# First layer's turns as integers and q's second order on ScalarE, block inputs in their own buffer, later first blocks and no saved credit in a fused attention and two-layer kernel

## The chip, the cores and the metric

The kernel runs on one core of a Trainium2 chip. The metric is the device time of one execution in microseconds. The core has TensorE (PE in the rows: matmuls; PEld: its weight loads), VectorE (DVE), ScalarE (ACT), GpSimd (POOL) and SyncE (SP), whose queue issues every DMA of this kernel, one after the other.

## What is computed

An attention with queries that are the means of neighbouring pairs, then two dense layers. The weights arrive in double width (64 bit), q, k and v in single, and the output is single.

```python
def reference(q, k, v, w_in1, w_out1, w_in2, w_out2):   # B, H, S, D = 4, 8, 1152, 64
    qp = q.reshape(B, H, S // 2, 2, D).mean(axis=3)
    s = qp @ k.transpose(0, 1, 3, 2) / np.sqrt(D)
    a = np.exp(s - s.max(-1, keepdims=True))
    x = (a / (a.sum(-1, keepdims=True) + 1e-9)) @ v       # to rows of 8 * 64 = 512
    h = x @ w_in1;  x = (h * np.cos(h)) @ w_out1          # 512 -> 2048 -> 512
    h = x @ w_in2;  return (h / (1 + np.exp(-h))) @ w_out2
```

## The kernel before

Every product of near single precision is made from half-precision parts: a number is split into a high part and the rest (the second order), and three products are summed. Splits are ScalarE (high part), then VectorE or POOL (the rest).

The attention runs over 4 batches of 4 pairs of heads (heads j and j + 4), and each pair has 9 tiles of 128 queries (the ninth holds 64 of either head): 144 tiles. A tile goes through TensorE (`tile_scores`), VectorE (eviction with the minimum, L568, L573), ScalarE (exponential, L576, and its high part, L582), POOL (the rest, L150, three pieces), one transpose by DMA of both parts (L589, hlT) and TensorE again (`tile_pv`, L600 and L604). The ring of `hl` has 4 buffers, scores have one PSUM buffer for each of their two halves, and the second product of a tile follows 4 tiles later (`LAG`).

The next pair is prepared meanwhile. `pair_prep` finds scales and splits q, k and v; it and the loads (`pair_loads`) are generators of which the tile loop takes a step every second call of `advance` (four calls a tile, 36 a pair). For q, `qn` holds four column sets: for e = 0 the high part beside the rest, for e = 1 the rest beside the high part (the two halves of the contraction meet k's high part and rest). All of it goes through one DMA transpose (L515), as k does (L525).

When a batch is done its 512 whole rows are two blocks of 256 tokens; its remaining 64 rows wait for a ninth block. `block_steps` scales and splits a block (`x_split`, whose `xn` is a buffer of the ring `hl`), transposes it (xT) and puts it into `blocks_q`, in batches 1 to 3 only 40 calls of `advance` (10 tiles) later.

`layer1` is a generator of units. For each chunk f of 128 of the 2048 columns there is one unit of 12 matmuls into PSUM (`g1_unit`; two chunks share a buffer, of which there are two), and 12 chunks later one for the second product (`g2_unit1`). After each second chunk ScalarE evicts two chunks as turns, h / 2 pi, into `hk` (L701). After each fourth, VectorE makes the turns' distance to the nearest whole number: add a quarter, add and subtract 1.5 * 2^23 (L713, L714, into a buffer of the tag `tt`). ScalarE takes the sine (L720), VectorE multiplies and rounds (L723, L728), POOL makes the rest (L150, gl). A block's output y32 takes a buffer of `tt`, too, and goes to DRAM (L752). `tt`, `hk`, `gh` and `gl` have two buffers each.

`share` runs units: each call adds a credit, of which at most 4 are kept, and every unit costs one. A tile makes two calls in batches 1 to 3. After the last tile the rest of the first layer runs with the preparation of the second layer's weights (`layer2_weight_steps`); then the second layer's blocks follow, by TensorE mostly.

The framework orders all instructions by a list scheduler over modelled times, with the program's order and hand-set priorities (`ahead`) as keys; each engine then runs its own list in order.

Of the kernel before, what the change touches and what calls it, by code (L numbers as in the profile page):

```python
# [20 lines left out]
EXP_MASK = 0x7F800000  # L21
MAGIC = 12582912.0
TINY = 2.0**-50
# [3 lines left out]
PSH = 15.0  # L27
NB_N, NB_SC, NB_H, NB_T, NB_S = 2, 4, 4, 4, 5
LOW_HL, LOW_G, LOW_W = 3, 2, 2
X_LAG = 40  # L30
W1_BUFS, WT_BUFS = 3, 3
# [18 lines left out]
def attention_moe_moe_kernel(ctx, tc, q, k, v, w_in1, w_out1, w_in2, w_out2, out):  # L50
# [23 lines left out]
    halfpi = const.tile([128, 1], F32, name="halfpi")  # L74
    floor3 = const.tile([128, 1], F32, name="floor3")

    def make_consts():
        nc.vector.memset(mean, 2.0**-7)
        nc.vector.memset(halfpi, math.pi / 2)
        nc.vector.memset(floor3, 2.0**-14 - 0.5)  # L80

    GW = 256
# [390 lines left out]
    def pair_prep(at, P):  # L473
# [32 lines left out]

        qn = at.src.tile([128, 2, NQ, 2, D], F16, tag="kn", name="qn", bufs=NB_N)
        for e in range(2):
            nc.scalar.activation(out=qn[:, e, :, e, :], in_=qs, func=AF.Copy, scale=s[:, 0:1])
        nc.vector.scalar_tensor_tensor(  # L510
            out=qn[:, 0, :, 1, :], in0=qs, scalar=s[:, 0:1], in1=qn[:, 0, :, 0, :], op0=ALU.mult, op1=ALU.subtract
        )
        nc.vector.tensor_copy(qn[:, 1, :, 0, :], qn[:, 0, :, 1, :])
        qT = at.p.tile([128, 2, NQ, 128], F16, tag="qT", name="qT", bufs=2)
        nc.sync.dma_start_transpose(  # L515
            out=qT.rearrange("p e n k -> p (e n) k"), in_=qn.rearrange("p e n s d -> p (e n s d)")
        )
        P.qT = [qT[:, e] for e in range(2)]
        yield
        kn = at.src.tile([128, 2, KC, 2, D], F16, tag="kn", name="kn", bufs=NB_N)  # L520
        for i in range(2):
# [8 lines left out]
        for i in range(2):  # L530
            do_v(i)
            yield

    segs = [(o, min(512, S - o)) for o in range(0, S, 512)]
# [122 lines left out]
    def x_split(at, mp, x32, i, blk, w):  # L657

        m = small.tile([128, 1], F32, name="xm", tag="xm")
        absmax(m, x32, AX.XY)  # L660
        yield
        s = small.tile([128, 1], F32, name="xs", tag="xs")
        u = small.tile([128, 1], F32, name="xu", tag="xu")
        yield from early(scale_steps(m, ps_h, (s, u), 14), P_CH)
        blk.c = x_scale_consts(w, s, u, True)
        xn = at.p.tile([128, 2, 2, DM], F16, tag="hl", name="xn", bufs=NB_H)
        nc.scalar.activation(out=xn[:, 0], in_=x32, func=AF.Copy, scale=s)
        nc.vector.scalar_tensor_tensor(out=xn[:, 1], in0=x32, scalar=s, in1=xn[:, 0], op0=ALU.mult, op1=ALU.subtract)
        yield
        blk.T = mp.p.tile([128, 2, 2, NC, 128], F16, tag="x%d" % i, name="xT", bufs=1)  # L670
        nc.sync.dma_start_transpose(
            out=blk.T.rearrange("p e t c k -> p (e t c) k"), in_=xn.rearrange("p e t d -> p (e t d)")
        )
        blk.xh = lambda c: blk.T[:, 0, :, c, :]
        blk.xl = lambda c: blk.T[:, 1, :, c, :]
# [15 lines left out]
    def g1_evac(mp, w, blk, f, first):  # L691
# [3 lines left out]
        if first:  # L695
            if f % 4 == 1:
                blk.hk = mp.p.tile([128, 4, GW], F32, tag="hk", name="hk", bufs=NB_HK)
            o = blk.hk[:, (f % 4) - 1:(f % 4) + 1, :]
        else:
            o = blk.view(f - 1, 2)  # L700
        nc.scalar.activation(  # L701
            out=o, in_=blk.hp, func=AF.Copy if first else AF.Silu, scale=blk.c.a[:, g:g + 1]
        )

    def g_cos_begin(mp, blk):
# [5 lines left out]
        blk.g.append((G.gh, G.gl))  # L711
        G.t = t = mp.p.tile([128, 4, GW], F32, tag="tt", name="tt", bufs=NB_TT)
        nc.vector.tensor_scalar(out=t, in0=G.hk, scalar1=0.25, scalar2=MAGIC, op0=ALU.add, op1=ALU.add)  # L713
        nc.vector.scalar_tensor_tensor(out=t, in0=t, scalar=MAGIC, in1=G.hk, op0=ALU.subtract, op1=ALU.subtract)  # L714
        return G
# [165 lines left out]
    if True:  # L881
# [12 lines left out]
        state = Weights()  # L894
        state.mp = None
        state.ng, state.tail = 0, False
# [51 lines left out]
        def share(x):  # L948
            if state.mp is None:
                return  # L950
            state.credit = min(state.credit + x, 4.0)
            while state.credit >= 1 and next(units, False):
                state.credit -= 1
# [31 lines left out]
        def block_steps(b, i):  # L985
# [3 lines left out]
            yield from early(x_split(at, state.mp, x32.pop((b, i)), i, blk, W1), P_X)  # L989
            if b:  # L990
                for _ in range(X_LAG):
                    yield
            blocks_q.append(blk)
# [8 lines left out]
        def block_done(b, i):  # L1002
            if state.mp is None:
                finish(wg)
                wst_stack.close()
                state.mp = moe_pools(moe_stack)
            xgens[b, i] = block_steps(b, i)
            bg.append(xgens[b, i])
# [41 lines left out]
        for n, (b, j) in enumerate(pairs):  # L1050
# [13 lines left out]
            else:  # L1064
                at.src_stack.close()
                w2st_stack = ExitStack()
                w2st = w2st_stack.enter_context(tc.tile_pool(name="w2st", bufs=1, reuse_waits="tile"))
# [203 lines left out]
```

## Time and profile before

| | us |
|---|---|
| median of 3 runs | 1358.67 (1353.96 to 1359.51) |
| the profiled execution, own time | 1361.32 |
| its span, first to last instruction | 1359.5 |
| mean granted clock of TensorE | 0.916 |
| end of the attention in it | about 829 |
| TensorE without a gap from | about 1059 |

The profile gives the busy time of each engine, the windows its distribution over time, and the groups what each line costs and what ended the idle time before it. A wait is named by engine and line, with the releaser behind an arrow. DMA share is the mean busy share of the 16 DMA engines.

### The profile page before, as it was taken

The page shows a single profiled execution, that of the slowest core. Times are in us where ns is not written, and L with a number is a line of the kernel's source. Part 1 is how long each engine was busy: PE and PEld are TensorE (multiplying, and loading weights), DVE is VectorE, ACT ScalarE, POOL GpSimd, SP SyncE. Part 2 cuts the span into 40 slices and gives each one's busy share as a digit, 9 for nine tenths or more (in the row PEclk, how much of TensorE's full clock was granted, in tenths as well). Part 3 has the DMA queues.
Part 4 walks back from the last instruction along what each step waited for, and adds up shares of the span by engine and source line. Part 5 has one row for each costly group of instructions (what it writes and reads, how often), then busy time and mean ns, then how long its engine had stood idle before and what let it go on. Part 6 is the DMA issues. An engine that isn't in the chain of part 4 may idle for free. (4 is left out here: it accounts for less than half of the span.)

```text
span 1359.5 us, 26737 instructions
## 1 busy us (share of the span) xinstructions
PE 1146.0 (84%) x10668; PEld 914.5 (67%) x10668; DVE 981.6 (72%) x1927; ACT 870.0 (64%) x1061; POOL 705.1 (52%) x624
## 2 busy tenths in 40 slices
PE   1564565888988679998898999899999999999998
PEld 0333343666766456675676677788788888888887
DVE  6896978877877777795787795986757755444483
ACT  3896888778777777885788774634546633333352
POOL 1688686688668576875768673533667400000000
PEclk9677676989999888998999999999899999999999
DMA  9999999889799999998999975413344000000001
GB/s 270 210 229 219 224 242 208 152 159 175 139 191 186 195 201 202 191 162 161 164 181 190 197 174 100 128 60 75 82 97 106 32 30 27 9 16 17 17 32 32
DMA packets 509597, 186.29 MB, mean 137 GB/s; under 512 B 465952, under 2 KB 484384, under 8 KB 509472
## 3 DMA queue, kind: packets, MB, share of 16 engines
q1 hardware_dynamic: 509472, 184.59, 65.7%
q8 instruction: 83, 1.36, 0.4%
q14 instruction: 42, 0.34, 0.1%
HBM read 66.58 MB, written 9.44 MB: 56 GB/s over the span
## 5 line engine op out<-in xcount | busy, mean ns | idle before, releaser
L150 POOL TENSOR_TENSOR hl<-sc,hl 128x384 f16<-128x384 f32 x432 | 453.8, 1081 | 145.3 <-ACT hl L582 110.1
L568 DVE TENSOR_SCALAR_CACHE_REDUCE sc<-sp,psu 128x512 f32<-128x512 f32 (+1 forms) x288 | 229.7, 808 | 78.1 <-PE sp L549 66.9
L549 PE MATMUL sp<-kT,qT 128*128 128x512 f16 (+1 forms) x768 | 195.3, 373 | 83.5 <-DVE sc L568 58.7
L685 PEld LDWEIGHTS <-ih 128*128 128x128 f16 x2304 | 226.3, 100 | 45.7 <-issue 13.8
L600 PE MATMUL pv<-vt,hlT 128*128 128x130 f16 (+1 forms) x1440 | 194.6, 236 | 73.8 <-DMA hlT<-hl 68.2
L576 ACT ACTIVATE sc<-sc,nb 128x1152 f32<-128x1152 f32 x144 | 179.4, 1249 | 76.8 <-DVE nb L573 69.7
L600 PEld LDWEIGHTS <-hlT 128*128 128x128 f16 (+1 forms) x1440 | 144.6, 109 | 106.3 <-DMA hlT<-hl 80.9
L685 PE MATMUL h<-ys,ih 128*128 128x256 f16 x1152 | 195.6, 274 | 4.1 <-ACT gs L701 4.1
L685 PE MATMUL h<-xT,ih 128*128 128x256 f16 x1024 | 186.3, 277 | 5.1 <-ACT hk L701 2.1
L604 PE MATMUL pv<-vt,hlT 128*128 128x65 f16 (+1 forms) x1440 | 184.7, 206 | 0.0
L582 ACT ACTIVATE hl<-sc 128x1152 f16<-128x1152 f32 x144 | 165.2, 1154 | 26.2 <-DMA hlT<-hl 20.0
L549 PEld LDWEIGHTS <-qT 128*128 128x128 f16 x768 | 77.1, 109 | 150.9 <-issue 102.5
L740 PE MATMUL y<-gh,oh 128*128 128x256 f16 x576 | 162.8, 283 | 6.8 <-ACT y L749 6.8
L740 PE MATMUL y<-gl,oh 128*128 128x256 f16 x576 | 163.1, 283 | 1.9 <-POOL gl L150 1.9
L740 PE MATMUL y<-gh,ol 128*128 128x256 f16 x576 | 162.6, 282 | 0.0
L854 PEld LDWEIGHTS <-op 128*128 128x128 f16 x1512 | 147.9, 98 | 18.0 <-issue 0.6
L685 PE MATMUL h<-ys,il 128*128 128x256 f16 x576 | 157.7, 274 | 0.0
L604 PEld LDWEIGHTS <-hlT 128*128 128x128 f16 (+1 forms) x1440 | 141.2, 107 | 14.6 <-issue 7.1
L685 PE MATMUL h<-xT,il 128*128 128x256 f16 x512 | 141.8, 277 | 0.0
L150 POOL TENSOR_TENSOR gl<-tt,gh 128x512 f16<-128x512 f32 (+1 forms) x60 | 97.3, 1637 | 79.7 <-DVE gh L728 61.0
L740 PEld LDWEIGHTS <-oh 128*128 128x128 f16 x1152 | 115.4, 102 | 30.8 <-issue 10.3
L685 PEld LDWEIGHTS <-il 128*128 128x128 f16 x1152 | 114.2, 99 | 16.9 <-issue 0.4
(310 smaller groups left out, 1967.6 us busy)
## 6 DMA issues: line engine op xcount, KB each, us to landing
wst<-in_moe_w_in_dram SPq DMA_DIRECT2D x16, 1024.0 KB, 6.1
stk<-in_k_dram SPq DMA_DIRECT2D x32, 288.0 KB, 4.2
stv<-in_v_dram SPq DMA_DIRECT2D x32, 288.0 KB, 4.4
stq<-in_q_dram SPq DMA_DIRECT2D x32, 256.0 KB, 3.1
wst<-in_moe_w_out_dram SPq DMA_DIRECT2D x8, 1024.0 KB, 6.4
wst<-in_moe_w_out_dram SPq DMA_DIRECT2D x16, 512.0 KB, 6.0
ydr<-y SPq DMA_DIRECT2D x9, 512.0 KB, 3.3
y32b<-ydr SPq DMA_DIRECT2D x9, 512.0 KB, 3.3
```

The source lines that it names most:

```text
L150: last = nc.gpsimd.tensor_tensor(out=lo[:, o:o + w], in0=x[:, o:o + w], in1=hi[:, o:o + w], op=ALU.subtract)
L549: nc.tensor.matmul(sp[:, o - a:o - a + n], P.qT[e][:, t, :], kT[:, o:o + n], start=(e == 0), stop=(e == 1))
L568: nc.vector.tensor_scalar(out=T.sc[:, a:z], in0=sp, scalar1=T.P.su, scalar2=None, op0=ALU.mult, op1=ALU.min, accum_out=mx[:, x:x + 1],)
L576: nc.scalar.activation(out=T.sc, in_=T.sc, func=AF.Exp, scale=-1.0, bias=nb)
L582: nc.scalar.activation(out=hi, in_=T.sc, func=AF.Copy)
L600: nc.tensor.matmul(G.pv[r, T.gi], T.hlT[:, 0, c, r], P.vt[i][:, c], start=(c == 0), stop=(c == KC - 1), skip_group_check=True,)
L604: nc.tensor.matmul(G.pv[r, T.gi, 0], T.hlT[:, 1, c, r], P.vt[i][:, c, 0], start=False, stop=(c == KC - 1), skip_group_check=True,)
L685: nc.tensor.matmul(hp, wt[:, c, f * 128:(f + 1) * 128], xt(c), start=(i == 0), stop=(i == 3 * NC - 1), skip_group_check=True,)
L740: nc.tensor.matmul(blk.y[:, oc, :], wt[:, f, oc * 128:(oc + 1) * 128], gt[:, f % 4, :], start=(f == 0 and e == 0 and oc % 2 == 0), stop=(f ...
L854: nc.tensor.matmul(bank, t[:, e, c, :], wt[:, c, :], start=start, stop=True, skip_group_check=True)
```

## The change

- `g1_evac` reads each PSUM buffer of the first layer twice: as before into `hk`, and with a quarter added, converted to 32-bit integers, into a buffer of `tt` that is now claimed at the second chunk of four. VectorE's two instructions become one, integer minus turns.
- `qn` holds q's high part and rest once, in a buffer of its own, and the transpose takes 9 blocks, not 18. The e = 1 half of `qT` is made from the e = 0 half by two ScalarE copies that swap the upper and lower 64 partitions, as a last step of `pair_prep`. `kn` has one buffer.
- `xn` has a buffer in a pool of its own, as long as that pool is open (until the last pair of batch 3 begins; there the steps of batch 2's blocks are finished first). After that it uses `hl` as before.
- `X_LAG` is 20 calls for batch 0 (before: none) and 40 for the others.
- When `share` finds no unit to run, the credit is set to 0.

```diff
-        qn = at.src.tile([128, 2, NQ, 2, D], F16, tag="kn", name="qn", bufs=NB_N)
-        for e in range(2):
-            nc.scalar.activation(out=qn[:, e, :, e, :], in_=qs, func=AF.Copy, scale=s[:, 0:1])
-        nc.vector.scalar_tensor_tensor(
-            out=qn[:, 0, :, 1, :], in0=qs, scalar=s[:, 0:1], in1=qn[:, 0, :, 0, :], op0=ALU.mult, op1=ALU.subtract
-        )
-        nc.vector.tensor_copy(qn[:, 1, :, 0, :], qn[:, 0, :, 1, :])
+        qn = at.src.tile([128, NQ, 2, D], F16, tag="qn", name="qn", bufs=1)
+        split(qn[:, :, 0, :], qn[:, :, 1, :], qs, s[:, 0:1], False)
         qT = at.p.tile([128, 2, NQ, 128], F16, tag="qT", name="qT", bufs=2)
-        nc.sync.dma_start_transpose(
-            out=qT.rearrange("p e n k -> p (e n) k"), in_=qn.rearrange("p e n s d -> p (e n s d)")
-        )
+        nc.sync.dma_start_transpose(out=qT[:, 0], in_=qn.rearrange("p n s d -> p (n s d)"))
...
-        kn = at.src.tile([128, 2, KC, 2, D], F16, tag="kn", name="kn", bufs=NB_N)
+        kn = at.src.tile([128, 2, KC, 2, D], F16, tag="kn", name="kn", bufs=1)
...
+        for x, y in ((slice(0, 64), slice(64, 128)), (slice(64, 128), slice(0, 64))):
+            nc.scalar.activation(out=qT[x, 1], in_=qT[y, 0], func=AF.Copy)
+        yield
...
-        xn = at.p.tile([128, 2, 2, DM], F16, tag="hl", name="xn", bufs=NB_H)
+        if state.xp is None:
+            xn = at.p.tile([128, 2, 2, DM], F16, tag="hl", name="xn", bufs=NB_H)
+        else:
+            xn = state.xp.tile([128, 2, 2, DM], F16, name="xn", bufs=1)
...
+                blk.tt = mp.p.tile([128, 4, GW], F32, tag="tt", name="tt", bufs=NB_TT)
...
+        if first:
+            nc.scalar.activation(
+                out=blk.tt.bitcast(I32)[:, (f % 4) - 1:(f % 4) + 1, :], in_=blk.hp, func=AF.Identity,
+                scale=blk.c.a[:, g:g + 1], bias=quarter,
+            )
...
-        G.t = t = mp.p.tile([128, 4, GW], F32, tag="tt", name="tt", bufs=NB_TT)
-        nc.vector.tensor_scalar(out=t, in0=G.hk, scalar1=0.25, scalar2=MAGIC, op0=ALU.add, op1=ALU.add)
-        nc.vector.scalar_tensor_tensor(out=t, in0=t, scalar=MAGIC, in1=G.hk, op0=ALU.subtract, op1=ALU.subtract)
+        G.t = t = blk.tt
+        nc.vector.tensor_tensor(out=t, in0=t.bitcast(I32), in1=G.hk, op=ALU.subtract)
...
             state.credit = min(state.credit + x, 4.0)
-            while state.credit >= 1 and next(units, False):
+            while state.credit >= 1:
+                if not next(units, False):
+                    state.credit = 0.0
+                    return
                 state.credit -= 1
...
-            if b:
-                for _ in range(X_LAG):
-                    yield
+            for _ in range(X_LAG[b > 0]):
+                yield
             blocks_q.append(blk)
```

## Rows read from the trace of the kernel before

**Rows 1.** Page, part 1: busy us (share of the span) xinstructions

```profile
PE 1146.0 (84%) x10668; PEld 914.5 (67%) x10668; DVE 981.6 (72%) x1927; ACT 870.0 (64%) x1061; POOL 705.1 (52%) x624
```

**Rows 2.** Windows: us, PE, PEld, DVE, ACT, POOL busy (x), PEclk, DMA share, GB/s

```profile
37.00:228.00 191.00, 110.44 (x908) 70.07 (x907) 157.38 (x368) 159.26 (x179) 142.31 (x129) 0.68 1.04 222
...
290.00:610.00 320.00, 272.15 (x2701) 202.32 (x2700) 248.50 (x545) 250.62 (x297) 229.43 (x215) 0.93 0.96 181
...
650.00:829.00 179.00, 159.85 (x1650) 123.39 (x1648) 144.79 (x295) 139.89 (x168) 134.83 (x120) 0.97 0.95 180
...
829.00:1059.00 230.00, 213.79 (x1864) 185.84 (x1865) 165.20 (x247) 114.43 (x151) 117.98 (x78) 0.95 0.37 90
```

**Rows 3.** TensorE group, 37 to 228 us: busy, mean ns | idle before

```profile
L600 PE MATMUL pv<-vt,hlT 128*128 128x130 f16 x252 | 38.6, 268 | 43.0 <-DMA hlT<-hl 40.0 <-DVE uo L112 1.8 <-DVE pvs L618 1.0
```

**Rows 4.** Windows of 5 us, 460 to 600: first and last of 28

```profile
460.00:465.00 5.00, 5.00 (x56) 4.17 (x55) 4.97 (x11) 5.00 (x8) 0.00 (x0) 1.00 1.29 184
...
595.00:600.00 5.00, 5.00 (x58) 4.09 (x56) 4.64 (x11) 4.98 (x6) 2.61 (x3) 1.00 1.01 186
```

**Rows 5.** One piece of the chain: start, us, what

```profile
1287.43 1.31 PE h L685 x12
```

**Rows 6.** VectorE groups of the whole run, by shape

```profile
L713 DVE TENSOR_SCALAR tt<-hk 128x1024 f32<-128x1024 f32 x36 | 32.1, 890 | 17.1 <-ACT hk L701 15.8 <-DMA ydr<-y 0.8 <-ACT hl L582 0.4
...
L779 DVE TENSOR_TENSOR gs<-s,gs 128x1024 f32<-128x1024 f32 x7 | 8.5, 1221 | 0.1
...
L513 DVE COPY qn<-qn 128x576 f16<-128x576 f16 x16 | 7.3, 456 | 0.1
```

**Rows 7.** Timeline of POOL and VectorE after the attention

```profile
856.62 2.42 POOL L150 TENSOR_TENSOR gl<-tt,gh 128x1024 f16<-128x1024 f32 x1 [0.72 <-DVE gh L728]
...
857.09 3.03 DVE L714 SCALAR_TENSOR_TENSOR tt<-tt,hk 128x1024 f32<-128x1024 f32 x1
```

**Rows 8.** ScalarE groups of 240 to 820 us, by shape

```profile
L576 ACT ACTIVATE sc<-sc,nb 128x1152 f32<-128x1152 f32 x106 | 132.3, 1250 | 58.1 <-DVE nb L573 52.5 <-DVE den L616 2.7 <-DVE xs L116 1.7
...
L582 ACT ACTIVATE hl<-sc 128x1152 f16<-128x1152 f32 x107 | 122.7, 1155 | 13.6 <-DMA hlT<-hl 7.4 <-DMA xT<-xn 5.1
...
L701 ACT ACTIVATE hk<-h,ca 128x512 f32<-128x512 f32 x48 | 32.2, 674 | 13.4 <-PE h L685 13.4
```

**Rows 9.** The instructions on tile qn: ns min/median/max, first and last start

```profile
L515 SPq DMA_TRANSPOSE qT<-qn x16: 2697/2839/3931, 17.1 to 747.9; - x16
...
L509 ACT ACTIVATE qn<-stq,ps__162 x2: 759/768/776, 14.9 to 15.6; 128x576 f16<-128x576 f32 x2
```

**Rows 10.** Page, part 6: DMA issues, KB each, us to landing

```profile
stk<-in_k_dram SPq DMA_DIRECT2D x32, 288.0 KB, 4.2
...
ydr<-y SPq DMA_DIRECT2D x9, 512.0 KB, 3.3
```

**Rows 11.** Who waited on tile xT: us, times

```profile
  ACT hl L582: 5.1, 2
```

**Rows 12.** Timeline of VectorE where batch 0's first block enters

```profile
259.65 0.75 DVE L568 TENSOR_SCALAR_CACHE_REDUCE sc<-sp,psu 128x512 f32<-128x512 f32 x1 [4.85 <-PE sp L549]
```

**Rows 13.** Timeline of SP and TensorE, start: start us, us, engine

```profile
17.14 3.93 SPq L515 DMA_TRANSPOSE qT<-qn  x1
...
25.81 2.08 PE L549 MATMUL sp<-kT,qT 128*128 128x512 f16 x6 [12.66 <-DMA kT<-kn]
```

**Rows 14.** One window of 20 us after the attention

```profile
880.00:900.00 20.00, 20.00 (x186) 17.93 (x184) 19.97 (x19) 4.84 (x6) 6.64 (x3) 1.00 0.17 54
```

**Rows 15.** Timeline of ScalarE and SP: first and last of five block outputs

```profile
373.25 0.67 ACT L701 ACTIVATE hk<-h,ca 128x512 f32<-128x512 f32 x1
...
382.20 0.52 SPq L752 DMA_DIRECT2D ydr<-y  x1
...
806.50 0.70 ACT L701 ACTIVATE hk<-h,ca 128x512 f32<-128x512 f32 x1
...
806.66 0.34 SPq L752 DMA_DIRECT2D ydr<-y  x1
```

More of the change, by code (lines that the diff above doesn't have):

```diff
@@ L21 @@
 EXP_MASK = 0x7F800000
-MAGIC = 12582912.0
 TINY = 2.0**-50
@@ L27 @@
 PSH = 15.0
-NB_N, NB_SC, NB_H, NB_T, NB_S = 2, 4, 4, 4, 5
+NB_SC, NB_H, NB_T, NB_S = 4, 4, 4, 5
 LOW_HL, LOW_G, LOW_W = 3, 2, 2
-X_LAG = 40
+X_LAG = (20, 40)
 W1_BUFS, WT_BUFS = 3, 3
@@ L75, in attention_moe_moe_kernel @@
     floor3 = const.tile([128, 1], F32, name="floor3")
+    quarter = const.tile([128, 1], F32, name="quarter")
     def make_consts():
@@ L80, in make_consts @@
         nc.vector.memset(floor3, 2.0**-14 - 0.5)
+        nc.vector.memset(quarter, 0.25)
     GW = 256
@@ L894, in attention_moe_moe_kernel @@
         state = Weights()
-        state.mp = None
+        state.mp = state.xp = None
+        xn_stack = ExitStack()
         state.ng, state.tail = 0, False
@@ L1006, in block_done @@
                 state.mp = moe_pools(moe_stack)
+                state.xp = xn_stack.enter_context(tc.tile_pool(name="xn", bufs=1, reuse_waits="tile"))
             xgens[b, i] = block_steps(b, i)
@@ L1065, in attention_moe_moe_kernel @@
                 at.src_stack.close()
+                for i in range(2):
+                    finish(xgens[b - 1, i])
+                xn_stack.close()
+                state.xp = None
                 w2st_stack = ExitStack()
```

## The prediction

> **What bounds the kernel now.** I read the busy shares of the page first [rows 1]: no engine is full over the span, so the limits must differ by stage. The windows by stage [rows 2] show them. From 37 to 228 us (batch 0's attention, no first layer beside it) the DMA share is 1.04, and TensorE lost 40.0 us there waiting for transposed weights hlT [rows 3]: a DMA stage. From 290 to 829 us (batches 1 to 3 with the first layer woven in) VectorE and ScalarE stand together at 78% (248.5 and 250.6 of 320 us) beside a DMA share of 0.96: no single bound. The windows of 5 us say how these shares lie in time [rows 4] (there the first and the last of the 28): ScalarE is over 4.9 of 5 us in 13 of the 28, VectorE in 12, the DMA share is at 1.0 or more in 17. After 829 us DMA falls to 0.37, TensorE has 213.8 of 230 us and VectorE 165.2. From about 1059 us the chain is TensorE alone, 12 matmuls in 1.31 us each time [rows 5], and nothing in the change reaches that part except through when it starts.
>
> The profiled execution took 1361.3 us (span 1359.5); the median of three runs is 1358.7, 2.6 lower. I add to 1361.3 and take 2.6 off at the end.
>
> **The change, part by part.**
>
> Integer turns. Gone: 36 tensor_scalar of 890 ns on VectorE, 32.1 us [rows 6]. The subtraction stays as one VectorE instruction with two SBUF operands; a tensor_tensor of that size took 1221 ns [rows 6]. The one that it replaces took 3.03 us where POOL worked beside it, and ended just after POOL's 2.42 us did [rows 7]. I count no gain for it (the other end would be a gain of some 0.4 us each, 14 us). The Trainium skill, SBUF — State Buffer, section "Who interferes with whom", says that a VectorE instruction with two SBUF inputs blocks against GpSimd's reads and that the first to issue wins; rows 7 agree. By that rule the new instruction waits as the old one did, and the sum is the same.
>
> Added: 72 ScalarE reads of PSUM with scale and bias. The like of it with a scale alone took 674 ns; a bias operand cost 1250 - 1155 = 95 ns on 1152 columns [rows 8]. So 0.77 us each, 55 us; bounds 0.67 and 0.86. 48 of them come before 820 us (that row's count), 24 after. The Trainium skill, ScalarE: Activation LUTs, section "Rules for kernel authors", speaks against this edit: it wants adds and multiplies on VectorE. The rows agree on the price: two reads of 0.77 us replace one VectorE pass of 0.89. By that rule alone the edit loses 0.65 us a group; what it loses in time is rival 3's question.
>
> q's second order. Gone for each of 16 pairs: one ScalarE pass of 0.76 us [rows 9], one VectorE copy of 0.456 us [rows 6], and half of the transpose's 18 blocks. SP is held 2.84 us by the whole one [rows 9], so 1.42 us of the queue that carries every transfer. No row shows a transpose of 9 blocks: the bounds are no gain and 2.0 us. Added: two ScalarE copies across partitions, 1152 columns on 64 lanes. Nearest row: 1155 ns for 1152 columns on 128 lanes [rows 8]; as none crosses partitions I allow 0.9 to 1.5. Net on ScalarE +1.55 us a pair. They wait for the transpose: what is queued behind on ScalarE are the next tiles' exponentials. The cover: prep now has 13 steps of 2 advances, 26 of a pair's 36, so 10 advances (2.5 tiles) lie between them and the first scores. The same extra step makes all loads of the next pair 2 advances later; k's first load keeps 6 advances of about 1.4 us (144 tiles of 4 advances from 37 to 829 us), 8.4 us, before VectorE reads it, and it lands in 4.2 [rows 10]. I cost it at nothing; without cover it would be 2.8 us a pair, 34 us for 12 pairs.
>
> Own buffers. kn loses its second buffer; a pair lies between its uses, nothing. xn leaves the ring of hl, where ScalarE waited 5.1 us in two cases for an xT transpose [rows 11].
>
> Entry of blocks. Batch 0's blocks enter 5 tiles later, and a wait for blocks no longer piles up 4 credits. Now, when the first block enters, 4 units (5.2 us of TensorE) go ahead of the scores, and VectorE waits 4.85 us for these [rows 12]. With one credit the wait shrinks to some 1.3 us. The five tiles cost nothing in the first layer, which before batch 1's blocks has no work for over ten tiles. By the loops' own counts the three entries lose 3 units each; the first two are made good in those gaps, the third leaves 3 units (172 against 169 before the inflight tiles end) for the tail: 3 x 1.31 = 3.9 us [rows 5].
>
> The sum by stage:
> - Start: the k transpose queues behind the q one, which held SP 3.93 us, and the first scores waited 12.66 us for kT [rows 13]. Half of 3.93 and the copy of 0.46: -2.5 (0 to -3).
> - Batch 0: 4 more q transposes at 1.42 in a stage full of DMA: -5 (0 to -8).
> - Batch 0's blocks: 4.85 less 1.3, and half of the 5.1: -6 (0 to -10).
> - Batches 1 to 3, 12 pairs: VectorE 24 x 0.89 + 12 x 0.456 = 26.9 us less; ScalarE 48 x 0.77 + 12 x 1.55 = 55.6 us more; SP 12 x 1.42 = 17 us less. What lies on the path is estimated from the shares of full windows: -26.9 x 12/28 = -11.5, +55.6 x 13/28 = +25.8, -17 x 17/28 = -10.3: +4 (-22, if ScalarE's idle time takes all its work, to +25).
> - Tail: 12 groups x 0.89 = 10.7 us off VectorE, which fills single windows there (19.97 of 20 us) [rows 14] but not the stage; taken -3 (0 to -10.7). ScalarE's 24 x 0.77 find 115 idle us [rows 2]. With the 3.9 of the units: +1.
>
> Together -8.5: 1352.8, less 2.6: **1350 us**.
>
> **The rivals.**
> 1. ScalarE's added work falls into its idle time (70 of 320 us [rows 2]), so only the relief counts: -22 in batches 1 to 3 in place of +4, 1324 us. For it: 58.1 us of ScalarE's idle time before exponentials end with VectorE's minimum [rows 8], the engine that is relieved. Against: ScalarE is full as often as VectorE.
> 2. The change does not bring what it says at the entries: the order of instructions is made anew by a scheduler from modelled times, and the scores may stand behind units again; then half of the 13.5 us of the first three terms is lost: 1357 us.
> 3. Slower: the buffers of the turns. There are two; a group claimed one at its fourth chunk, and VectorE waited for it. Now ScalarE claims it at the second. A block's output y32 takes one of the two while the other is held by the group before it, and gives it back only when its transfer has landed. So the second read of chunk 13 waits for that transfer, with exponentials behind it. First and last of the five block outputs before the attention ends: chunk 13 evicted at 373.25, transfer issued at 382.20 [rows 15] and landed 3.3 us later [rows 10], 12.3 us; 806.50 and 806.66, 3.5 us. Mean 7.9, five times: 39 us if ScalarE stands for all of it, about 20 if other work is put before it in half of the time: 1350 + 20 = 1370 us. It decides as soon as SP issues the transfer later than ScalarE reaches chunk 13; SP is in order, and transposes that wait for POOL stand before it. Against: the reads can be placed later, and PSUM has a second buffer for two chunks.
>
> **How the numbers follow.** Forecast 1350 (1341 to 1357, with the bounds of the small terms): 0.36. Rival 1: 0.20, rival 2: 0.18, rival 3: 0.26. A measurement of this kernel tells about 0.5% from no change, 1351.9 to 1365.5. Faster: rival 1, and six tenths of the forecast's cases and a little of rival 2's, 0.44. Slower: rival 3 and the worst of rival 2, 0.28. The same: 0.28. The range takes in rival 1's time with its widest relief and rival 3 with three quarters of its wait: 1320 to 1378. Cases of both signs have weight; the forecast's own range is 1341 to 1357.
>
> **What would show it.** Right: no tensor_scalar on the turns, VectorE down by 39 us (32.1 + 7.3) and ScalarE up by about 80 (55 + 16 x 1.55) on the page; first scores near 23.3 us; no wait near 4.9 us of VectorE on scores at the first block's entry; 37 to 228 us shorter with TensorE's wait for hlT below 40. Wrong: idle time of ScalarE before the integer read that ends with a ydr transfer or POOL's gl (rival 3); ScalarE idle time gone and VectorE waiting for its exponentials less (rival 1). The forecast falls if the attention's end (829 us) moves by over 15 us either way, or if the tail from there grows by over 6 us.

## The result and the profile after

The changed kernel takes **1339.5 us** (median of four runs, 1335.4 to 1344.3) against 1357.0 us for the kernel before on the same chip: a ratio of 0.9874, 95% interval 0.9826 to 0.9921. It is faster by 1.3%. The forecast was 1350; the time lies inside the range (1320 to 1378) and under the forecast's own (1341 to 1357). The profiled execution took 1335.4 us, its span 1333.7 (before 1359.5). The four executions fall into two groups, 1335.4 and 1336.1 us at a mean granted clock of TensorE of 0.933 and 0.934, and 1342.9 and 1344.3 us at 0.922 and 0.923. The profile before is of an execution 4.4 us above its median, the profile after of one 4.1 below, so their rows lie 25.9 us apart where the medians lie 17.5 apart.

The page's first part, kernel after, answers [rows 1]:

```profile
PE 1126.1 (84%) x10668; PEld 906.7 (68%) x10668; DVE 957.4 (72%) x1876; ACT 941.0 (71%) x1149; POOL 706.9 (53%) x624
```

ScalarE rose by 71.0 us (80 were forecast) and VectorE fell by 24.2 (39 were forecast). The windows by stage, kernel after, answer [rows 2]; their columns are the same (the attention now ends at about 790 us, so the last two windows don't hold the same work as before):

```profile
37.00:228.00 191.00, 108.14 (x909) 69.25 (x910) 164.75 (x368) 165.01 (x182) 147.90 (x133) 0.70 1.02 218
290.00:610.00 320.00, 281.36 (x2819) 213.71 (x2817) 240.46 (x529) 279.50 (x339) 227.02 (x212) 0.95 0.91 177
650.00:829.00 179.00, 164.31 (x1728) 132.25 (x1728) 135.75 (x284) 150.58 (x185) 125.81 (x108) 0.98 0.86 171
829.00:1059.00 230.00, 207.80 (x1858) 182.56 (x1857) 164.56 (x226) 132.64 (x178) 121.25 (x82) 0.98 0.32 77
```

From 290 to 610 us ScalarE is now at 279.5 of 320 us (250.6 before), the DMA share has gone from 0.96 to 0.91, and TensorE did more matmuls in the same time (2819, before 2701). The new and replaced instructions, groups of the whole run, kernel after (busy us, mean ns | idle time of the engine before them, and what ended it):

```profile
L706 ACT ACTIVATE tt<-h,quarter,ca 128x512 int32<-128x512 f32 x72 | 55.0, 770 | 12.7 <-POOL gl L151 7.7 <-DMA ydr<-y 5.0
L719 DVE TENSOR_TENSOR tt<-tt,hk 128x1024 f32<-128x1024 int32 x36 | 55.3, 1537 | 19.8 <-ACT tt L706 19.7
L528 ACT ACTIVATE qT<-qT 64x1152 f16<-64x1152 f16 x32 | 37.2, 1162 | 7.9 <-DMA qT<-qn 7.4
```

The integer read costs 0.770 us, as summed. The rival with the turns' buffer is real, with both of its named releasers (POOL's gl and the ydr transfer), but it is worth 12.7 us of ScalarE's idle time and not up to 39. Of these, 10.3 us come after the last tile's high part, all of the waits for ydr among them, where no exponentials stand behind the read. The longest of those:

```profile
795.02 0.78 ACT L706 ACTIVATE tt<-h,quarter,ca 128x512 int32<-128x512 f32 x1 [4.36 <-DMA ydr<-y]
```

The copy across partitions took 1.16 us, inside the 0.9 to 1.5.

**Where the time went.** The kernel has 16 pairs (4 batches of 4). I take as a pair's start the start of the first of its nine ScalarE copies of high parts, and as the attention's end the start of the last of the 144. In us of the span, worked out from the rows of that line in the two profiles (differences taken before rounding):

```
                    before   after    difference
pair 0 starts         32.8    29.3    -3.5
batch 0 lasts        199.6   200.6    +1.1
batch 1 lasts        201.6   196.0    -5.6
batch 2 lasts        186.1   186.4    +0.3
batch 3 lasts        198.0   177.2   -20.8
from there to the end 541.5  544.2    +2.6
```

Most of it lies in batch 3. The pieces scatter by some microseconds from kernel to kernel: batch 0, which holds no first layer, lasts 200.6 us here and 202.3 to 205.6 in the seven runs below that leave its work as in the changed kernel. This table alone would suggest that the entry of the blocks did what the forecast wanted of it (-6 forecast, -5.6 measured in batch 1). The runs say otherwise.

### The profile page after: what moved, and what is told of

Same layout as the page of the kernel before. It is cut to its first block, busy times and chain, and to the rows that moved or that the text cites. A ratio compares the mean times of both kernels' runs of the same rounds, so it can differ in the third digit from the quotient of the medians.

```text
span 1333.7 us, 26712 instructions
## 1 busy us (share of the span) xinstructions
PE 1126.1 (84%) x10668; PEld 906.7 (68%) x10668; DVE 957.4 (72%) x1876; ACT 941.0 (71%) x1149; POOL 706.9 (53%) x624
## 5 line engine op out<-in xcount | busy, mean ns | idle before, releaser
L565 DVE TENSOR_SCALAR_CACHE_REDUCE sc<-sp,psu 128x512 f32<-128x512 f32 (+1 forms) x288 | 228.8, 807 | 55.6 <-PE sp L546 43.6
L546 PE MATMUL sp<-kT,qT 128*128 128x512 f16 (+1 forms) x768 | 200.1, 373 | 77.7 <-DVE sc L565 65.5
L597 PEld LDWEIGHTS <-hlT 128*128 128x128 f16 (+1 forms) x1440 | 145.8, 109 | 90.2 <-DMA hlT<-hl 49.8
L745 PE MATMUL y<-gh,oh 128*128 128x256 f16 x576 | 158.5, 275 | 9.9 <-ACT y L754 9.8
L745 PE MATMUL y<-gl,oh 128*128 128x256 f16 x576 | 158.5, 275 | 0.0
L745 PE MATMUL y<-gh,ol 128*128 128x256 f16 x576 | 158.3, 275 | 0.0
L745 PEld LDWEIGHTS <-oh 128*128 128x128 f16 x1152 | 112.0, 99 | 30.1 <-issue 13.7
```

The source lines that it names most:

```text
L546: nc.tensor.matmul(sp[:, o - a:o - a + n], P.qT[e][:, t, :], kT[:, o:o + n], start=(e == 0), stop=(e == 1))
L565: nc.vector.tensor_scalar(out=T.sc[:, a:z], in0=sp, scalar1=T.P.su, scalar2=None, op0=ALU.mult, op1=ALU.min, accum_out=mx[:, x:x + 1],)
L597: nc.tensor.matmul(G.pv[r, T.gi], T.hlT[:, 0, c, r], P.vt[i][:, c], start=(c == 0), stop=(c == KC - 1), skip_group_check=True,)
L745: nc.tensor.matmul(blk.y[:, oc, :], wt[:, f, oc * 128:(oc + 1) * 128], gt[:, f % 4, :], start=(f == 0 and e == 0 and oc % 2 == 0), stop=(f ...
```

## The experiments

The theories at the start: **entry** (the blocks' later entry brings the gain), **relief** (VectorE and SP are relieved, and ScalarE's added work falls into its idle time) and **order** (the scheduler makes the whole order anew, and parts don't add up). All times are medians; each ratio is to the kernel before on the same chip, with its 95% interval. A half, here and in the expectations, is what the prediction calls a unit: 12 matmuls of the first layer, one half of a chunk's work. Six blocks (batches 0 to 2) have 192 of them that can run before the attention ends.

**1. Each part undone.** The turns back on VectorE:

```diff
-            nc.scalar.activation(out=blk.tt.bitcast(I32)[...], in_=blk.hp, func=AF.Identity, scale=..., bias=quarter)
+        nc.vector.tensor_scalar(out=t, in0=G.hk, scalar1=0.25, scalar2=MAGIC, op0=ALU.add, op1=ALU.add)
...
```

> The changed kernel (median 1339.5 us) with the turns made by VectorE's two instructions again, all else as changed. Theory E (the gain of 17.5 us is the new entry of blocks: later first blocks, no saved credit): 1337 to 1343, no matter where the turns are made; VectorE +32 us of tensor_scalar, ScalarE -55. Rival R (the gain is VectorE's relief, with ScalarE's added work in its idle time): 1350 or more, with the attention's end back by over 10 us from its 789.5 (last high part of a tile). Rival O (the order that the scheduler makes anew decides): any value from 1335 to 1357 with stalls at other places than in the changed kernel.

Measured 1334.5 us, 0.983 (0.9792 to 0.9867). With all else changed, the turns' edit gives nothing; it may cost 5 us.

q's second order back as it was (a transpose of 18 blocks, second copy made before it):

```diff
-        nc.sync.dma_start_transpose(out=qT[:, 0], in_=qn.rearrange("p n s d -> p (n s d)"))
+        nc.sync.dma_start_transpose(out=qT.rearrange("p e n k -> p (e n) k"), in_=qn.rearrange("p e n s d -> p (e n s d)"))
...
```

> The changed kernel with q's second order by VectorE and the transpose of 18 blocks again, all else as changed. Theory E: 1339 to 1344 (the first scores about 2.5 to 4 us later, and nothing beside that). Rival R: 1345 or more, since SP gets back 1.4 us in each of 16 pairs and VectorE 0.46. Rival O: any value, with stalls elsewhere.

Measured 1349.1 us, 0.9935 (0.9917 to 0.9953): this edit is worth about 10 us here (the two intervals allow 1 to 15). It shows in TensorE's wait for hlT (weight loads of the line of the matmuls on it; the kernel before, then after, then this run):

```profile
L600 PEld LDWEIGHTS <-hlT 128*128 128x128 f16 (+1 forms) x1440 | 144.6, 109 | 106.3 <-DMA hlT<-hl 80.9 <-issue 15.8 <-DMA stk<-in_k_dram 0.2
```

```profile
L597 PEld LDWEIGHTS <-hlT 128*128 128x128 f16 (+1 forms) x1440 | 145.8, 109 | 90.2 <-DMA hlT<-hl 49.8 <-issue 31.0
```

```profile
L601 PEld LDWEIGHTS <-hlT 128*128 128x128 f16 (+1 forms) x1440 | 147.1, 110 | 119.8 <-DMA hlT<-hl 91.6 <-issue 18.3
```

With the long transpose back, the wait is back, from 49.8 to 91.6 us. But most of it does not set the time. The same wait in batch 0 alone (29.3 to 229.9 us after, 30.5 to 230.9 in this run; us in total, times, longest):

```profile
PEld L597 <- DMA hlT<-hl: 28.1, 15, 3.8
PEld L601 <- DMA hlT<-hl: 58.4, 26, 5.6
```

30.3 of the 41.8 us lie in batch 0, which lasts 200.4 us in this run and 200.6 in the changed kernel. The time is lost at the start (1.2 us) and in batches 1 to 3 (8.6 us), where the wait differs by the other 11.5 us. That hlT's own transposes stand behind q's on SP's queue there was not followed and is not shown.

Both halves of the entry edit undone:

```diff
-X_LAG = (20, 40)
+X_LAG = (0, 40)
-            while state.credit >= 1:
-                if not next(units, False):
-                    state.credit = 0.0
-                    return
+            while state.credit >= 1 and next(units, False):
                 state.credit -= 1
```

> The changed kernel with batch 0's blocks entering at once and with the saved credit, all else as changed. Theory E: back to 1352 to 1359, with VectorE waiting about 5 us for scores behind the first block's 4 units. Rival R: 1337 to 1343. Rival O: any value, with stalls elsewhere.

Measured **1324.7 us**, 0.9752 (0.9712 to 0.9792): 15 us faster than the whole change. Batch 1 lasts 196.8 us, as good as after's 196.0. The theory "entry" falls: in this kernel the entry edit costs 15 us, and batch 1 stays as short without it.

**2. The parts alone, in the kernel before.** Both halves of the entry edit:

> The kernel before with the two edits of the entry alone (20 calls of lag for batch 0, credit set to 0 when no unit is there). Theory E: 1338 to 1345. Rival R: 1352 to 1358. Rival O: any value; then e3 and e4 do not add up to the gain.

Measured 1349.2 us, 0.9933 (0.9907 to 0.996). So the same edit gains 9 us in one kernel and costs 15 in the other. Batch 1, where the blocks enter, lasts 200.5 us here, against 201.6 before.

q alone:

> The kernel before with q's edit alone: half transposes of 9 blocks, and q's second-order rows copied by ScalarE. Undoing this edit in the changed kernel cost 9.6 us (1349.1 against 1339.5). Theory relief: the same gain by itself, 1345 to 1350 against 1358, PEld's wait for hlT down from 80.9 us to about 55. Theory order: the parts don't add up, 1350 to 1362, and the wait for hlT down without the time following.

Measured 1338.6 us, 0.9851 (0.9809 to 0.9894), 21 us, twice what undoing it cost; the wait for hlT fell to 49.9 us, and batch 1 lasts 196.0 us. The turns alone:

> The kernel before with the turns' edit alone: ScalarE makes the integer turns (72 reads of 770 ns, 55 us of its time), VectorE loses the magic-number pass. Undoing this edit in the changed kernel gave 1334.5 against 1339.5. Theory relief with hidden work (ScalarE's reads lie in its idle time, VectorE is relieved): 1345 to 1352 against 1358. Theory charge (ScalarE's reads delay exp and the high parts, as the forecast summed it): 1357 to 1365, exp starting later behind the maximum. Theory order: between 1345 and 1370 with no sign.

Measured 1344.6 us, 0.9901 (0.9867 to 0.9936), 15 us: relief with hidden work. Batch 1 lasts 196.1 us. The whole-run rows of the exponentials, the kernel before and then this one:

```profile
L576 ACT ACTIVATE sc<-sc,nb 128x1152 f32<-128x1152 f32 x144 | 179.4, 1249 | 76.8 <-DVE nb L573 69.7 <-DVE den L616 4.1 <-DVE xs L116 1.7
```

```profile
L577 ACT ACTIVATE sc<-sc,nb 128x1152 f32<-128x1152 f32 x144 | 179.2, 1249 | 62.3 <-DVE nb L574 45.0 <-DVE den L617 11.5 <-DVE xs L117 4.1
```

ScalarE's wait for VectorE's minimum (nb) fell by 24.7 us: time in which it can do a part of the 55 us of integer reads.

The lag alone (credit still saved):

```diff
-X_LAG = 40
+X_LAG = (20, 40)
-            if b:
-                for _ in range(X_LAG):
-                    yield
+            for _ in range(X_LAG[b > 0]):
+                yield
```

> The kernel before with the lag alone (the first batch's blocks enter 5 tiles later; credit is still saved). With both halves of the entry edit the kernel before ran at 1349.2, 9 us under its own time. In the changed kernel the lag moved nothing (1324.3 with it, 1324.7 without it, both with saved credit) and the missing credit cost 15 us. Theory credit always costs: the lag alone gives more than the pair, 1335 to 1345. Theory lag does nothing: 1354 to 1362, and the pair's 9 us came from the missing credit. Theory order: anything between.

Measured 1347.0 us, 0.992 (0.9891 to 0.9949). That lies between the two expectations: the 9 us of the entry edit in the kernel before are the lag's (11 us by itself), and the credit's half neither adds to them nor takes much from them. Where they come from is another matter: batch 1 lasts 202.3 us in this run, and the gain is in batches 2 and 3 (3.5 and 8.7 us).

Groups 1 and 2 together hold every combination of the three edits. Times in percent of the kernel before on the same chip; the upper row is the kernel before, entry alone, turns alone and q undone, the lower one q alone, turns undone, entry undone and the whole change (the runs of group 1 and the whole change also hold the block inputs' own buffer, which group 3 finds worth nothing):

```
                        neither    entry     turns     both
q as before             100.00     99.33     99.01     99.35
q's second order new     98.51     98.30     97.52     98.74
```

The intervals are 0.2 to 0.5 to either side. In both rows the turns gain 1.0 without the entry edit and nothing with it (0.0 and -0.4), and in both rows the entry edit does better without the turns (gains of 0.7 and 0.2) than beside them (losses of 0.3 and 1.2). q gains in every column. So it is these two edits that don't go together, whatever q does.

**3. Which half of the entry edit costs 15 us.** Saved credit, lag kept:

> The changed kernel with the saved credit put back in the planner (the first layer's units may again pile up what they were not granted); the later entry of the first batch's blocks (5 tiles) is kept. Undoing both halves of the entry edit gave 1324.7 against the changed kernel's 1339.5, with all of the gain behind attention's end. Theory credit (the missing credit leaves more units for the tail): about 1325, and the time from the last high part to the end near 532 us instead of 544. Theory lag (the 5 tiles do it): 1337 to 1342, tail near 544. Theory order (any edit of the list makes a new order, worth up to 15 us either way): anything from 1322 to 1350, with a tail that follows neither.

Measured **1324.3 us**, 0.9748 (0.9702 to 0.9793), the best time of all, and equal to the run without the lag. So in this kernel it is the credit, as that theory said; its tail is 535.9 us (532 expected), and 8.4 us of the gain lie in the attention, which it didn't expect.

Is any edit of the order worth as much? One more tile of lag (20 to 24; the expectation names the wrong one of the two numbers):

> The changed kernel with the second number of the lag that the first batch's blocks have to the first layer changed by one (24 and 40 tiles become another pair of values in the same planner call, nothing else). No instruction is added or taken away, only the due times of the first layer's units move. It measures how much a time moves by order alone. Theory relief (the engines' amounts of work set the time): 1337 to 1342, as the changed kernel. Theory order: a move of 5 to 15 us to either side, 1325 to 1355, all of it at places where an engine waits for an operand that the new order makes late.

Measured 1337.8 us, 0.9868 (0.981 to 0.9926), as the changed kernel. This one disturbance of the order moves nothing, which speaks for a cause of the 15 us of their own; one such run can't rule out an accident of the order.

The block inputs back in the ring of hl, on top of saved credit:

```diff
-        if state.xp is None:
-            xn = at.p.tile([128, 2, 2, DM], F16, tag="hl", name="xn", bufs=NB_H)
-        else:
-            xn = state.xp.tile([128, 2, 2, DM], F16, name="xn", bufs=1)
+        xn = at.p.tile([128, 2, 2, DM], F16, tag="hl", name="xn", bufs=NB_H)
```

> The changed kernel with saved credit (1324.3) and the block inputs put back in the buffers of the high parts (hl). It prices the buffer of their own. The forecast gave the first entry of blocks 4.9 us for it, and the same wait stands at the later entries. Theory buffer (the high parts' buffers are held by the inputs until their transposes land, and ScalarE and SP wait): 1329 to 1340. Theory sum (the two edits q and turns, 21 and 15 us by themselves, carry all of it): 1320 to 1328.

Measured 1325.1 us, 0.9756 (0.9723 to 0.9789) against 1324.3: their own buffer is worth nothing that can be measured.

**4. Is the number of halves left behind the attention the cause?** The kernels with saved credit had 178.6 to 179.9 halves done at the attention's end, those whose credit expires 175.8 to 177.0 (matmuls of the two lines before that moment, by 12). If the attention hides what it takes in, more should help. With saved credit, the pending second halves are emitted while the first layer waits for a block:

```diff
                         while not blocks_q:
-                            yield False
+                            if pend:
+                                g2_next()
+                                yield True
+                            else:
+                                yield False
...
```

> The changed kernel with saved credit, and one more edit of the planner: while the first layer waits for a next block, its up to 12 pending second halves are emitted and not held. Theory count (what decides behind attention is how many halves of units, of 12 matmuls and 3.3 us each, are left when it ends; attention hides them in TensorE's waits): of the 192 halves that six blocks have, more than the 183 of the kernel with saved credit are done at attention's end, each worth up to 3.3 us: 1300 to 1320. Theory full attention (attention has no more room, what is moved in makes it longer): 1322 to 1332, with attention's end later by what the tail loses. Credit is the cap: where the planner has none left, the count stays at 183 to 185 and the time at 1322 to 1327.

Measured 1347.8 us, 0.9934 (0.9898 to 0.997). 188.1 halves were done at the attention's end, and that end came at 807.5 us in place of 781.1; the tail was 534.9 in place of 535.9. So the count is not what decides, and "full attention" is right, by more than it said. (Two figures in the expectation are off: 183 is the count at 800 us of the kernel with the whole entry edit undone, and at the attention's end it is 179.8 there and 179.2 with saved credit and the lag; and 3.3 us adds up the records of 12 pipelined matmuls, which TensorE passes in 1.31 us [rows 5].) The same with more credit:

```diff
-RATE = (0, 2, 2, 2)
+RATE = (0, 2.5, 2.5, 2.5)
```

> As the run before it, with 2.5 instead of 2 half units of credit for each tile in batches 1 to 3, so that credit isn't the cap. Theory count: all or nearly all of the 192 halves are done by attention's end, 1295 to 1315. Theory full attention: the more units stand between the scores, the later these come; 1325 to 1345, with attention's end later by over 10 us.

Measured 1375.3 us, 1.0136 (1.0107 to 1.0166), slower than the kernel before. All 192 halves were done, at an attention's end of 843.6 us.

**What the fourth group shows instead.** These two kernels alternate between pairs crammed with halves and pairs without. I counted the halves in each of pairs 4 to 14 in all 14 kernels (154 pairs) and set them beside the pair's length:

```
halves in the pair   pairs   mean length us   shortest, longest
under 8                12        42.7            38.5, 47.2
8 to 12                20        45.4            33.7, 54.3
12 to 16               49        44.5            38.0, 51.9
16 to 18               40        49.5            42.7, 63.6
18 to 20               18        53.0            45.8, 59.3
20 and more            15        58.4            52.7, 63.3
```

Up to some 16 halves a pair's length hardly depends on them; above, each costs about 1.7 us (58.4 less 44.5 over the 8.0 halves between the means of the third and the last row; 2.0 without the last two runs), more than the 1.31 us of its own matmuls. Pairs differ in other things, too (those just after a batch also carry the preparation of its blocks), and the lengths in a row scatter by 10 us and more, so this is a tendency and not a proof. The windows fit it. Kernel after: pair 5 (19.9 halves), pair 8 (12.1), pair 10 (13.6) and pair 11 (19.0); columns as in [rows 2]:

```profile
271.10:328.50 57.40, 52.54 (x499) 38.36 (x497) 42.49 (x91) 53.17 (x61) 40.64 (x38) 1.00 0.87 177
425.90:468.50 42.60, 37.41 (x399) 28.49 (x397) 34.89 (x83) 37.19 (x43) 32.16 (x31) 0.96 1.07 192
518.40:558.80 40.40, 34.41 (x348) 26.71 (x345) 30.08 (x64) 35.49 (x41) 33.34 (x32) 0.92 1.06 193
558.80:612.30 53.50, 49.12 (x485) 36.77 (x484) 34.98 (x77) 43.34 (x54) 34.73 (x33) 1.00 0.74 148
```

The thin pairs run at a DMA share of 1.06 to 1.07, and by the table the halves in them are free. In the full ones TensorE is at 92% of the time and the DMA share is 0.74 to 0.87. By this reading two stages with different bounds stand one behind the other where they could overlap. Saved credit, pairs 8 to 11 (14.0, 14.3, 13.3 and 16.5 halves):

```profile
426.40:472.60 46.20, 41.66 (x443) 31.37 (x442) 36.29 (x94) 41.10 (x52) 29.67 (x30) 1.00 1.09 197
472.60:515.10 42.50, 36.87 (x388) 29.16 (x388) 31.38 (x69) 40.21 (x49) 31.33 (x30) 0.92 1.03 195
515.10:558.20 43.10, 34.66 (x364) 26.63 (x363) 35.20 (x82) 40.38 (x49) 33.12 (x32) 0.98 1.01 189
558.20:605.20 47.00, 44.49 (x456) 33.89 (x454) 36.77 (x82) 44.33 (x55) 36.81 (x35) 0.98 0.97 191
```

That batch does 58.1 halves in 178.8 us, where the changed kernel's does 55.3 in 186.4: the saved credit fills the thin pairs after a wait for blocks, the expired credit leaves them thin and the halves gather in pair 11. In the run with more credit it is plainest, pair 12 (6.0 halves) and pair 13 (26.7):

```profile
649.50:687.90 38.40, 30.80 (x299) 22.21 (x301) 30.77 (x78) 33.97 (x42) 25.95 (x28) 0.87 1.09 195
687.90:751.20 63.30, 55.08 (x563) 43.90 (x560) 48.17 (x95) 57.57 (x67) 47.78 (x39) 1.00 0.82 163
```

The last two runs bear the tendency out. Summed over the 12 pairs of batches 1 to 3, the halves above 16 in a pair are 9.3 with saved credit, 23.8 with the pending halves drained and 48.7 with more credit besides. At the 1.7 to 2.0 us of the table, these two should need 25 to 29 and 67 to 79 us more for the three batches; they need 29.7 and 63.7 (575.9 and 609.9 us against 546.2). They also do 9 and 13 halves more in all, but at 1.31 us these would be 12 and 17 us.

The credit's own cost is not explained by it. The changed kernel has 8.8 halves above 16, no more than the 9.3 of the kernel with saved credit, and yet needs 559.6 us for the three batches. Batch 2, shown above, is the one where its filling is the more uneven. With saved credit and no lag nothing is gained in the attention (7.3 halves above 16, its end at 790.75 us, 789.5 in the changed kernel), and the tail is 12.0 us shorter (532.2). Of those, the 4.0 halves that the changed kernel has more to do there are 5.2 us; the rest is slower work there (in its first 240 us TensorE is busy for 217.0 us at a granted clock of 0.98, in the other kernel for 221.5 at 0.99). Nor does expired credit alone make the long tail: with the turns undone it is 537.0 us, at 176.0 halves. Waits of TensorE over these 240 us, kernel after and then the kernel with saved credit and no lag (us in total, times, longest):

```profile
PE y L745 <- ACT y L754: 9.2, 3, 6.4
PE h L685 <- ACT gs L702: 8.7, 4, 4.9
```

```profile
PE h L685 <- ACT gs L702: 6.3, 4, 2.8
PE pv L597 <- DMA hlT<-hl: 3.1, 2, 2.0
PE y L745 <- ACT y L754: 2.7, 2, 1.7
```

TensorE waits there for ScalarE to empty a block's output, 9.2 against 2.7 us. The longest wait, 6.4 us, ends at 845.32 us, and ScalarE is at work through most of it:

```profile
839.30 1.15 ACT L725 ACTIVATE tt<-tt,halfpi 128x1024 f32<-128x1024 f32 x1 [0.39 <-DVE tt L719]
840.36 1.13 ACT L1124 ACTIVATE xnr<-xrem,srem 128x1024 f16<-128x1024 f32 x1
841.40 0.67 ACT L702 ACTIVATE hk<-h,ca 128x512 f32<-128x512 f32 x1
841.97 1.19 ACT L343 ACTIVATE ih<-wst,si 128x1024 f16<-128x1024 f32 x1
843.70 1.57 ACT L754 ACTIVATE y<-y,cy 128x256 f32<-128x256 f32 x4 [0.54 <-POOL gl L151]
```

Four other instructions stand before the one that TensorE needs. Why the scheduler's order comes out so with the expired credit and the integer turns together, and what the credit costs beyond the 5.2 us of the halves and the 6.5 us by which this wait differs, stays open.

## Why the prediction came out as it did

The time fell into the range because large errors of both signs cancelled. The sum by edit, worked out from its own terms, beside the edit alone in the kernel before:

```
edit                       in the sum    alone    with all others
integer turns               +5.0         -15.0    0 to +5
q's second order           -11.6         -21.0    -9.6
own buffer of the inputs    -2.6           -      -0.8
entry (lag and credit)      +0.4          -8.8    +14.8
```

(Turns: 24 x 0.89 x 12/28 of VectorE, 48 x 0.77 x 13/28 of ScalarE, and the 3 of the tail. The last column is the difference when the part is undone; for the inputs' buffer that was measured with saved credit.) Turns and q add up: alone they give 36 us, and the kernel that has both without the entry edit is 33.3 us under the kernel before. What doesn't add up is the entry edit beside the turns. The prediction had a sign of its own for this: the forecast falls if the attention's end moves by over 15 us either way. It moved by 28.5 us in the two profiles (31.3 us by the last product of the attention, 830.5 to 799.2). That the time lies in the range is luck.

**Start**: -2.5 forecast, -3.5 measured. The half transpose held SP for 1.64 us there (3.93 before), and the first scores came at 21.4 us, earlier than the 23.3 of the prediction:

```profile
21.41 0.59 PE L546 MATMUL sp<-kT,qT 128*128 128x512 f16 x1 [9.90 <-DMA kT<-kn]
```

**Batch 0**: -5 forecast, +1.1 measured; this step failed. The reading of the stage as DMA-bound rested on a share of 1.04 and on a wait for hlT of 40.0 us [rows 3]. That wait did fall, but another took its place. TensorE's groups from 37 to 228 us: the scores in the kernel before, then the scores and the hlT group after:

```profile
L549 PE MATMUL sp<-kT,qT 128*128 128x512 f16 x118 | 49.1, 526 | 19.9 <-DVE sc L568 17.2 <-DMA qT<-qn 2.4
```

```profile
L546 PE MATMUL sp<-kT,qT 128*128 128x512 f16 x120 | 51.4, 543 | 43.0 <-DVE sc L565 42.6
L597 PE MATMUL pv<-vt,hlT 128*128 128x130 f16 x259 | 37.5, 261 | 19.2 <-DMA hlT<-hl 13.3 <-DVE pvs L615 3.1 <-DVE den L613 2.5
```

The wait for hlT went from 40.0 to 13.3 us, and the wait for VectorE to empty the scores from 17.2 to 42.6. TensorE, at 108 of 191 us, is not what bounds this stage; its waits only change their name. What does bound it stays open: the DMA share is 1.02 with half of each q transpose gone, and VectorE and ScalarE are at 86%.

**Entry of batch 0's blocks**: -6 forecast, -5.6 measured, right in number and wrong in cause. VectorE's wait of 4.85 us [rows 12] is gone, but it is gone with the entry edit undone, too, while the lag alone in the kernel before has one of 6.1 us there:

```profile
270.98 0.75 DVE L568 TENSOR_SCALAR_CACHE_REDUCE sc<-sp,psu 128x512 f32<-128x512 f32 x1 [6.10 <-PE sp L549]
```

Batch 1 is as short with the entry edit undone (196.8 us), and as short with q alone or the turns alone (196.0 and 196.1); the entry edit alone and the lag alone leave it at 200.5 and 202.3. And the inputs' buffer, to which 2.55 of the 6 were given, is worth nothing measurable.

**Batches 1 to 3**: +4 forecast; batches 2 and 3 alone gave -20.5. The failed step is the price of ScalarE's added work: 55.6 us at 13/28, +25.8. A full 5-us window says that an engine was busy there, not that it is what the others wait for. The evidence for the first rival had been seen and outweighed: 58.1 us of ScalarE's idle time before exponentials [rows 8]. That group after, over the same 240 to 820 us:

```profile
L573 ACT ACTIVATE sc<-sc,nb 128x1152 f32<-128x1152 f32 x104 | 129.6, 1250 | 19.6 <-DVE nb L570 13.7 <-DVE den L613 4.2 <-DVE pm L488 1.2
```

The wait for the minimum fell from 52.5 to 13.7 us: the added work went where that rival put it. The Trainium skill, ScalarE: Activation LUTs, section "Rules for kernel authors", would have kept adds and multiplies on VectorE; here the edit gave 15 us alone, since the engine with idle time before its next step was ScalarE (and nothing beside the entry edit). The measurement decides, for this kernel.

**The subtraction on VectorE** was taken at no gain: 1602 ns before (57.7 us in 36), 1537 after.

```profile
L714 DVE SCALAR_TENSOR_TENSOR tt<-tt,hk 128x1024 f32<-128x1024 f32 x36 | 57.7, 1602 | 0.2
```

Its durations now run from 1206 to 3015 ns, and what parts them is whether a POOL instruction was running when it started: 13 of the 36 started with none running and took 1206 to 1225 ns, 23 started with one running and took 1717 in the mean (before: 15 at 1217 in the mean, 21 at 1877). The Trainium skill, SBUF — State Buffer, section "Who interferes with whom", says that a VectorE instruction with two SBUF inputs contends with GpSimd's reads; 1217 against 1717 ns agree. Ten of the 13 had a POOL instruction start while they ran and were not longer for it.

**Tail**: +1 forecast, +2.6 measured. The count that the prediction took from the loops, 3 units of 1.31 us, was near: 4.1 (179.9 less 175.8 halves). What it did not see is that the same rule could cost 15 us, almost four times its 3.9, beside the integer turns.

**The second rival** (the order eats the gain) was near in kind: one of three edits lost 15 us by when units are run, though not at the entry of a block, where the rival looked for it.

## What to carry to other kernels

Where filler work is woven between stages with another bound, spread it evenly: here up to some amount in each stage it cost hardly anything, above it was paid in full, and cramming it (the last two runs) cost 23 and 51 us against saved credit. Price work that is moved to another engine by that engine's idle time and by what ends it, not by how often its windows are full. And time the parts of a change by themselves, in pairs and undone: here two parts added up, and the third was a gain in the old kernel and a loss beside one of the two; without it (saved credit) the change takes 1324.3 us, 2.5% under the kernel before.

## What the runs showed of the hardware that was not expected

VectorE fell by 24.2 us where 39 were counted. 41.8 left the counted groups (32.1, 7.3 and 2.4). A part came back in instructions that the change doesn't touch, above all in the preparation of weights; the same line in the kernel before and after:

```profile
L322 DVE SCALAR_TENSOR_TENSOR wst<-wst,wt 128x1024 int32<-128x1024 int32 x16 | 21.4, 1337 | 0.1
```

```profile
L323 DVE SCALAR_TENSOR_TENSOR wst<-wst,wt 128x1024 int32<-128x1024 int32 x16 | 28.1, 1758 | 0.3
```

One shape took 1337 ns and then 1758 in the mean. Again what ran on POOL parts them: started with no POOL instruction running, all took 1209 to 1228 ns (12 of the 16 before, 6 after); started with one running, 1504 to 1861 before (4) and 1690 to 3151 after (10). The new order puts more of them beside POOL. So the busy time that this edit removed did not come off VectorE in full. The half transpose (9 blocks) held SP for 1.33 us against 2.84 for the whole [rows 9], so that cost went down with the number of blocks:

```profile
L511 SPq DMA_TRANSPOSE qT<-qn x16: 1282/1328/4022, 14.9 to 709.5; - x16
```
